# A recurrent attention and a GELU block in one launch: one list that orders all five queues is replaced by another

## The chip, the core and the metric

The kernel runs on one core of a Trainium2 chip. A core has five engines that matter here: TensorE (PE, matrix products; its weight loads are shown as PEld), VectorE (DVE), ScalarE (ACT), GpSimd (POOL) and SyncE (SP, which here only issues DMAs). Each engine works through a queue of its own, in order; semaphores hold an instruction until its inputs are there. The metric is the device time in microseconds (us) of one execution, the median over several runs.

## The reference, cut to what matters

```python
# r, k, v, w, a, b: (B, H, S, D) = (4, 8, 768, 40)
for t in range(S):
    y[:, :, t] = einsum('bhd,bhde->bhe', rt, state)
    Sa = einsum('bhde,bhe->bhd', state, at)
    state = state * wt[:, :, None, :] - einsum('bhd,bhe->bhde', Sa, bt)
    state = state + einsum('bhd,bhe->bhde', vt, kt)
x = y.transpose(0, 2, 1, 3).reshape(B * S, H * D)      # 3072 x 320
h = x @ w_in                                           # 320 x 2048
g = 0.5 * h * (1 + erf(h / sqrt(2)))
out = g @ w_out                                        # 2048 x 320
```

The two weights arrive as float64 and are converted to float32 on the chip.

## The kernel before, in words

**Tiling.** The sequence of 768 is cut into 12 chunks of 64 steps. Within a chunk the recurrence is turned into products: a triangular matrix is inverted, the state enters and leaves through products, and the 256 rows of y that a chunk gives (4 batches of 64) go through the GELU block at once. All products are in float32.

**Steps.** The kernel is written as about a hundred small functions, each marked as a step and each issuing instructions of mostly one engine. A token such as mh.3.6 calls step mh with the arguments 3 and 6; the first argument is the chunk, or the unit of a weight. `manual_schedule` is on for all five engines, so the order in which the steps are called is the order of the instructions on each engine's queue. That order is a list of 1450 tokens, written out in `order()` (line 19), and the kernel's last loop calls them one after the other:

```python
    for token in order(NCH, NS):
        perform(steps, token)
```

The list fixes the order of each queue only. Between queues the semaphores decide, and a step waits at the head of its queue for all that it reads and for the buffers that it writes.

**The steps that the text names**, with the engine and the line of the profile:
- Loads on SP: Lw, La, Lb, Lk, LV, Lr and others fetch a chunk's inputs (L447 to L515), Lf and Ls the weights (L537, L577).
- Weights, in units u (0 to 17 here): ce (two ACT instructions, L611 and L612), cs (two on DVE, L626 and L627), cm (DVE, L619) and cv (two on DVE, L635 and L636), in some units with cl, cn, cg, cx, cy in their place on other engines. A unit is usable after its cv.
- Decays: lg (ACT, L685, a logarithm), cu (PE), lt, ew, en, ec (ACT, exponentials and scalings), sb, sa, sk, sn (DVE or POOL) and the transposes ta, tb, tk, tv, tr (PE, or DVE as STREAM_TRANSPOSE). Chunks differ in the engine.
- The chunk's matrices: nm, vm, am (PE, L193), drained with a mask by nk, vk, ak (DVE); vc, rc, kc (ACT) drain transposes.
- The inverse: nd, nx, iz, then ic on POOL, about 30 us a chunk (L961, L963), then wx, tc_, wa, wb, and the products jm, km with the copies jc, kt0, kt1. For chunk 0 the inverse is made of squarings, qm on PE with qc, qb, qa, qz, qi on the other engines.
- The state: av, xm (PE), xc0 and xc1 (ACT or DVE copies, L1154), sm (PE), sc (DVE, L1175), pk, pb (PE), oa, od, om (DVE). oc, ot (ACT) and tn (DVE) turn the state for the next chunk; ym (PE) and yc (ACT, L1192 and L1194) give the part of y that comes from the old state.
- The GELU block: ox.c.0 and ox.c.1 move halves of y between partitions by five or six DMAs on SP (L1245, L1248). mh.c.p (PE, L1309) is one of eight products x @ w_in, with 20 matmuls; two of them fill a bank, which ge.c.q (ACT, L1314) reads with the GELU. For chunk 0, pm and pc multiply by w_out. From chunk 1 on, the product with w_out is made of seven products m1 to m7 (PE, L1348) with the sums ws, s1 to s4 (DVE), e1 to e6 (DVE and ACT). so and sz store the output through SP.
- Start: identity, sums_mask, upper_mask and the like set constants, most of them on POOL; warm and warm_first are products whose results nobody reads.

**PSUM.** Four tiles of two banks are handed out in the order of the list: a step on PE takes the tile that has been free longest, and the step that drains it gives it back. So the order of the drains on ACT and DVE decides when PE may go on.

```python
    def take(name, readers=1):
        held[name] = idle.pop(0)
    ...
    def drop(name):
        left[name] -= 1
        if not left[name]:
            idle.append(held.pop(name))
```

**ACT's tables.** A function of another kind than the one before needs a table load of 1.28 us on ACT (ACT_TABLE_LOAD in the profile); the order of the steps on ACT decides how many there are.

Of the kernel before, what the change touches and what calls it, by code (L numbers as in the profile page):

```python
# [18 lines left out]
def order(chunks, first_seven):  # L19
    return """  # L20
        first_ones.1 Lw.1 stripes_set identity pads_extra.1 sums_mask Lw.0 pads_r.1 warm.4.20 upper_mask
        pads_extra.3 La.0 pads_a.1 warm.4.0 pads_VR.1 pads_VR.0 of_half_set Lb.0 bias_set warm.4.13 pads_r.0 lg.1
        first_ones.0 pads_w.0 pads_rows.0 warm.4.25 pads_extra.0 Lb.1 pads_rows.1 onward_set lg.0 pads_w.1 wT.1
        pads_a.0 pads_extra.2 La.1 wT.0 warm.4.2 ew.1 Lf.0.1.0 ta.0 Lf.1.1.0 cu.0 Lf.0.0.0 cu.1 ec.0 Lf.1.0.0
        ew.0 sb.0 tb.0 sa.0 Lk.0 warm.4.15 sn.0 ec.1 nm.0 sb.1 Lf.2.0.0 warm_set tb.1 nk.0 Lf5.0.0 ta.1 sn.1 qt
        parity_set iz.1 sa.1 qm.0 qi.0.p qi.1.v nm.1 qz.0 warm_first ce.1 Lf.3.0.0 nk.1 qb.0.0.v Lf.3.1.0 qc.0
        cs.1 qb.0.1.a nd.1 qm.1 sk.0.p ce.0 nx.1 Lr.0 cm.1 Tt_zero tk.0 cs.0 cn.1 ic.1.0.4 qc.1 Lf.2.1.0 cl.1
        cx.1 qz.1 kc.0 Lf5.0.1 qb.1.0.v qa.1 qb.1.1.a cm.0 cy.1 ic.1.4.8 qm.2 Lf.0.0.1 cv.0 ce.3 LV.0 warm.4.18
        qz.2 am.0 qb.2.0.v qa.2 cs.3 ic.1.8.12 tr.0 Lf.1.0.1 ce.2 ak.0 Lw.2 qb.2.1.a cs.2 qc.2 Lf.0.1.1 rc.0 qm.3
        Lk.1 ic.1.12.16 Lf.2.0.1 qa.3 qz.3 Lf5.1.1 tv.0 qb.3.0.v qb.3.1.a cm.3 cm.2 cv.3 qm.4 vc.0 ic.1.16.20  # L30
        vm.0 qa.4 ql warm.4.4 vk.0 lg.2 Lf.2.1.1 ce.5 cv.2 av.0 Lf.3.1.1 ic.1.20.24 qc.3 qx jm.0 sk.1.v warm.4.24
        cs.5 Lf.1.1.1 cm.5 cv.5 Lf5.1.0 jc.0 km.0 xc0.0 xc1.0 ic.1.24.28 ce.7 Ls.3 cu.2 kt1.0 Ls.4 cs.7 kt0.0
        cm.7 sm.0 ic.1.28.31 cv.7 LV.1 ec.2 pk.0 sc.0.0 Lr.1 ce.9 sc.0.1 tk.1 cs.9 Lb.2 pb.0 kc.1 cm.9 cv.9 ce.4
        La.2 tv.1 om.0.1 om.0.0 Ls.2 cs.4 cm.4 Lf.3.0.1 vc.1 tr.1 od.0.1 cv.4 ox.0.0 am.1 rc.1 unused.v wT.2 ce.6
        sb.2 warm.4.1 one_set od.0.0 wx.1 ew.2 ta.2 ox.0.1 tb.2 sa.2 vm.1 sn.2 cs.6 cl.6 cm.6 nm.2 vk.1 oc.0 cn.6
        mh.0.0 nk.2 ot.0.1 cg.6 ot.0.0 ak.1 Ls.1 nd.2 Ls.0 nx.2 mh.0.1 iz.2 ce.8 tn.0 LV.2 unused.a mh.0.2 wb.1
        cs.8 ic.2.0.4 Lk.2 cm.8 cv.8 ge.0.0 av.1 Ls.6 ce.11 ym.1 ce.10 cs.11 ic.2.4.8 Ls.5 mh.0.3 tc_.1 Lr.2
        cm.11 yc.1 sk.2.v xm.1 cs.10 Ls.7 ge.0.1 cm.10 tv.2 ic.2.8.12 Ls.9 xc1.1 cv.10 xc0.1 Ls.10 jm.1 vc.2
        cv.11 Ls.8 tr.2 ce.12 tk.2 Ls.11 mh.0.6 ce.13 cs.12 ic.2.12.16 La.3 cm.12 kc.2 cs.13 mh.0.7 wa.1.1 cm.13
        jc.1 cv.12 rc.2 am.2 vm.2 cv.13 ic.2.16.20 ce.14 pm.0.0 Ls.13 cl.14 cs.14 Ls.12 ce.15 cm.14 ak.2 Lw.3  # L40
        cn.14 cs.15 km.1 wa.1.0 cg.14 vk.2 pm.0.1 kt1.1 ta.3 kt0.1 Ls.15 cm.15 Ls.14 cv.15 ic.2.20.24 ce.16 Lbt.3
        sm.1 ge.0.3 cs.16 ce.17 mh.0.4 sc.1.0 Lwt.3 sc.1.1 cl.17 ic.2.24.28 cm.16 mh.0.5 cs.17 Lr.3 cm.17 lg.3
        cv.16 pk.1 cn.17 cg.17 pb.1 ge.0.2 oa.1.0 cu.3 Lk.3 oa.1.1 pm.0.3 ec.3 od.1.0 Lw.4 ic.2.28.31 od.1.1 oc.1
        tw.3 ot.1.0 om.1.1 sk.3.p ot.1.1 om.1.0 av.2 tn.1 ox.1.1 pc.0.1 lt.3 ym.2 wx.2 iz.3 pm.0.2 tc_.2 yc.2
        unused.r pw.3 so.0.1 ew.3 tb.3 ox.1.0 jm.2 wb.2 en.3 pc.0.0 xm.2 jc.2 sn.3 km.2 xc0.2 tr.3 mh.1.0 xc1.2
        La.4 sa.3 wa.2.1 kt1.2 wa.2.0 nm.3 kt0.2 so.0.0 sm.2 nk.3 Lkt.3 mh.1.1 nd.3 sc.2.0 nx.3 lg.4 Lv.3 pk.2
        sc.2.1 ic.3.0.4 pb.2 ge.1.0 tk.3 mh.1.6 ic.3.4.8 oa.2.0 Lr.4 ta.4 mh.1.7 ws.0 LV.3 ws.1 mh.1.4 ge.1.3
        Lbt.4 ic.3.8.12 tr.4 mh.1.5 oa.2.1 Lk.4 kc.3 mh.1.2 tv.3 od.2.0 Lwt.4 ic.3.12.16 mh.1.3 od.2.1 oc.2
        om.2.0 vm.3 Lb.3 ge.1.1 am.3 ge.1.2 vk.3 m1.1 ot.2.1 ic.3.16.20 s1.1 ot.2.0 om.2.1 m2.1 s2.1 ox.2.1 ak.3
        m5.1 e1.1 tn.2 ws.3 av.3 e3.1 ic.3.20.24 s3.1 Lkt.4 ym.3 e2.1 tw.4 m6.1 yc.3 s4.1 ox.2.0 m3.1 ws.2 lt.4  # L50
        tk.4 m7.1 ic.3.24.28 e4.1 LV.4 tb.4 m4.1 e5.1 Lr.5 ic.3.28.31 xm.3 e6.1 pw.4 so.1.1 mh.2.6 xc0.3 La.5
        wx.3 ew.4 tc_.3 cu.4 sb.3 jm.3 en.4 so.1.0 mh.2.7 wb.3 sn.4 Lv.4 wa.3.0 jc.3 xc1.3 wa.3.1 km.3 sa.4 ec.4
        mh.2.4 sk.4.p tr.5 ge.2.3 kt1.3 Lkt.5 iz.4 ta.5 kt0.3 nm.4 sm.3 nk.4 Lw.5 mh.2.5 nd.4 nx.4 sc.3.0
        ic.4.0.4 mh.2.2 sc.3.1 Lbt.5 tv.4 mh.2.3 ic.4.4.8 kc.4 Lb.4 pk.3 ge.2.1 Lwt.5 ge.2.2 tb.5 pb.3 mh.2.0
        ic.4.8.12 sb.4 oa.3.1 oa.3.0 mh.2.1 od.3.0 om.3.1 am.4 ge.2.0 ic.4.12.16 om.3.0 vm.4 od.3.1 ox.3.1 m1.2
        s1.2 lg.5 tw.5 oc.3 ot.3.0 m2.2 s2.2 s4.2 m5.2 Lv.5 e1.2 vk.4 lt.5 ic.4.16.20 ot.3.1 s3.2 m6.2 ox.3.0
        ak.4 pw.5 m3.2 e3.2 ew.5 m7.2 La.6 e2.2 ic.4.20.24 tn.3 en.5 e4.2 m4.2 e5.2 av.4 e6.2 tk.5 so.2.1
        ic.4.24.28 ym.4 sn.5 Lr.6 mh.3.6 yc.4 sa.5 tv.5 LV.5 xm.4 ic.4.28.31 cu.5 xc1.4 xc0.4 mh.3.7 ec.5 wx.4
        tc_.4 wa.4.1 iz.5 ta.6 nm.5 ge.3.3 vm.5 Lbt.6 tr.6 wb.4 jm.4 nk.5 mh.3.2 jc.4 nd.5 Lwt.6 wa.4.0 nx.5
        mh.3.3 kc.5 ic.5.0.4 Lkt.6 vk.5 km.4 ge.3.1 mh.3.0 kt1.4 ic.5.4.8 kt0.4 tb.6 La.7 am.5 sm.4 tw.6  # L60
        ic.5.8.12 mh.3.1 lt.6 Lk.5 sc.4.1 sc.4.0 Lw.6 ak.5 mh.3.4 ge.3.0 pw.6 ic.5.12.16 mh.3.5 Lv.6 pk.4 ge.3.2
        s1.3 pb.4 so.2.0 lg.6 av.5 oa.4.1 ic.5.16.20 oa.4.0 m1.3 od.4.1 od.4.0 om.4.0 oc.4 m2.3 om.4.1 ot.4.0
        s2.3 ox.4.1 ot.4.1 ic.5.20.24 m5.3 tn.4 e1.3 s4.3 ew.6 ym.5 e2.3 s3.3 m6.3 yc.5 LV.6 tk.6 en.6 xm.5
        ic.5.24.28 ox.4.0 m3.3 xc0.5 ta.7 e4.3 sn.6 e3.3 m7.3 ic.5.28.31 Lk.6 sa.6 tv.6 Lb.5 m4.3 e5.3 Lbt.7 vm.6
        e6.3 nm.6 vk.6 mh.4.6 Lwt.7 nk.6 wx.5 wb.5 tc_.5 iz.6 mh.4.7 kc.6 nd.6 so.3.1 xc1.5 Lr.7 mh.4.2 nx.6 sb.5
        ic.6.0.4 ge.4.3 jm.5 am.6 jc.5 wa.5.1 km.5 wa.5.0 tw.7 sk.5.p mh.4.3 kt0.5 tb.7 ic.6.4.8 kt1.5 La.8
        mh.4.0 ak.6 ge.4.1 sm.5 Lb.6 ic.6.8.12 mh.4.1 sc.5.1 tr.7 pk.5 sc.5.0 ge.4.0 Lkt.7 ic.6.12.16 pb.5 lt.7
        cu.6 oa.5.1 Lw.7 mh.4.4 oa.5.0 pw.7 ic.6.16.20 mh.4.5 LV.7 om.5.1 m1.4 ge.4.2 Lv.7 od.5.0 om.5.0 s1.4
        m2.4 ec.6 ox.5.1 s2.4 ic.6.20.24 m5.4 od.5.1 ew.7 s3.4 en.7 s4.4 m6.4 oc.5 sn.7 ot.5.0 so.3.0 ot.5.1 m3.4
        sa.7 Lk.7 nm.7 e1.4 ox.5.0 ic.6.24.28 e3.4 e2.4 m7.4 e4.4 tn.5 m4.4 e5.4 ic.6.28.31 av.6 e6.4 nk.7 so.4.1  # L70
        sk.6.p ym.6 sb.6 wx.6 mh.5.6 wb.6 tv.7 iz.7 nd.7 tk.7 yc.6 mh.5.7 nx.7 Lr.8 wa.6.1 ic.7.0.4 vm.7 ge.5.3
        xm.6 Lwt.8 vk.7 mh.5.2 ic.7.4.8 xc0.6 ta.8 kc.7 Lbt.8 mh.5.3 xc1.6 tc_.6 tr.8 mh.5.0 ic.7.8.12 ge.5.1
        Lkt.8 tb.8 jm.6 lg.7 am.7 jc.6 Lb.7 wa.6.0 km.6 ic.7.12.16 tw.8 mh.5.1 so.4.0 kt1.6 ak.7 kt0.6 lt.8 Lv.8
        mh.5.4 pw.8 ic.7.16.20 ge.5.0 sm.6 mh.5.5 sc.6.0 sc.6.1 pk.6 ge.5.2 s1.5 pb.6 Lk.8 cu.7 oa.6.1 m1.5 La.9
        om.6.1 oa.6.0 ec.7 m2.5 sk.7.p od.6.0 om.6.0 s2.5 ox.6.1 m5.5 ic.7.20.24 e1.5 od.6.1 s3.5 oc.6 ew.8 m6.5
        s4.5 en.8 e2.5 m3.5 LV.8 e3.5 ot.6.0 e4.5 sa.8 ot.6.1 ox.6.0 m7.5 tn.6 ic.7.24.28 tk.8 m4.5 e5.5 Lr.9
        ic.7.28.31 av.7 e6.5 sb.7 sn.8 ym.7 so.5.1 mh.6.2 yc.7 wx.7 tc_.7 iz.8 Lb.8 xm.7 nm.8 mh.6.3 nk.8 nd.8
        tv.8 mh.6.6 xc1.7 Lwt.9 ge.6.1 nx.8 mh.6.7 kc.8 ic.8.0.4 Lw.8 vm.8 ge.6.3 am.8 xc0.7 vk.8 jm.7 ic.8.4.8
        wa.7.1 tw.9 mh.6.4 ta.9 lt.9 Lv.9 jc.7 pw.9 wb.7 mh.6.0 ic.8.8.12 lg.8 Lbt.9 wa.7.0 km.7 mh.6.1 kt1.7
        ak.8 kt0.7 ic.8.12.16 sm.7 ge.6.0 mh.6.5 sc.7.1 sc.7.0 tb.9 cu.8 ge.6.2 ic.8.16.20 Lw.9 pk.7 s1.6 pb.7  # L80
# [1388 lines left out]
```

## Time and profile before

| | |
|---|---|
| median of 3 runs | 647.54 us (647.45 to 648.93) |
| profiled execution, its own time | 648.82 us |
| its span | 646.9 us |
| TensorE busy | 617.4 us, 95% of the span |
| DVE, POOL, ACT busy | 457.3 (71%), 379.6 (59%), 323.9 us (50%) |
| mean granted TensorE clock | 0.99 |
| DMA | 64.3 MB, mean 99 GB/s |

A row of the time line gives the start and the duration in us, the engine, the line, the operation, what it writes and reads, the shape, and how often it stands in that row; in square brackets is the idle time of the engine before it and what ended that. A row of the windows gives the stretch, its length, the busy time of PE, PEld, DVE, ACT and POOL with the instructions, the granted clock, the share of the DMA engines and GB/s. A row of the groups gives the instructions of one line and form with their count, the busy time in us, the mean in ns, and the idle time before them. A row of the waits gives the engine and line that waited, what it waited for, the sum in us, how often, and the longest.

### The profile page before, as it was taken

What the parts mean: (1) busy time and instruction counts of PE and PEld (TensorE: products, weight loads), DVE (VectorE), ACT (ScalarE), POOL (GpSimd) and SP (SyncE); (2) the same over time, 40 slices, a digit from 0 to 9 for tenths busy, and PEclk for the clock granted to TensorE, in tenths of its full rate; (3) what the DMA queues carried; (4) which work ended last, traced back from release to release, by engine and by line L of the source; (5) the groups of instructions that cost most, each with busy time, mean ns of one, the idle gap of its engine ahead of it and who ended that gap; (6) DMA issues with size and microseconds to landing.
All of it is one profiled execution on the core that took longest, in us unless ns stands there. A gap on an engine that the chain in (4) does not pass through costs nothing.

```text
span 646.9 us, 31736 instructions
## 1 busy us (share of the span) xinstructions
PE 617.4 (95%) x14338; PEld 530.9 (82%) x14338; DVE 457.3 (71%) x557; ACT 323.9 (50%) x456; POOL 379.6 (59%) x782
## 2 busy tenths in 40 slices
...
GB/s 132 183 174 153 119 187 165 133 107 131 98 137 135 63 101 151 77 136 86 110 80 149 65 96 113 70 88 143 94 74 128 25 48 89 38 28 4 32 13 20
DMA packets 246914, 64.31 MB, mean 99 GB/s; under 512 B 228380, under 2 KB 243644, under 8 KB 246780
## 3 DMA queue, kind: packets, MB, share of 16 engines
...
q10 hardware_dynamic: 440, 0.29, 0.2%
q14 instruction: 22, 0.18, 0.1%
...
## 4 chain that ended last, share of the span: by engine, by line
PE 74%; issue 2%; ACT 2%; DVE 1%; DVEq 0%; ACTq 0%
PE bank L1309 29%; PE bank L1348 26%; PE bank L193 18%; DVE kT L721 0%; ACT L1314 0%; ACT L734 0%; ACT spare L922 0%; ACT T L942 0%; ACT Tt L937 0%; DVE spare L864 0%; ACT wpT L734 0%; ACT st L1194 0%; ACT kT L738 0%; ACT gt L1314 0%; DVE Tt L932 0%
## 5 line engine op out<-in xcount | busy, mean ns | idle before, releaser
L1309 PE MATMUL bank<-xt,w_in_sb 64*64 64x256 f32 x3840 | 224.5, 379 | 6.7 <-issue 6.0
L961 POOL TENSOR_TENSOR tmp<-W,Nb 128x126 f32<-128x126 f32 (+22 forms) x341 | 162.8, 478 | 95.3 <-DVE Nb L927 69.7
L1309 PEld LDWEIGHTS bank<-xt,w_in_sb 64*64 64x64 f32 x3840 | 161.3, 133 | 52.0 <-issue 11.1
L963 POOL TENSOR_TENSOR W<-W,tmp 128x126 f32<-128x126 f32 (+22 forms) x341 | 169.0, 496 | 26.7
L1348 PE MATMUL bank<-w_out_sb,gt 128*128 128x160 f32 x704 | 101.1, 301 | 0.0
L1314 ACT ACTIVATE gt<-bank 128x1024 f32<-128x1024 f32 x48 | 48.8, 1025 | 99.5 <-PE bank L1309 99.4
L1348 PEld LDWEIGHTS bank<-w_out_sb,gt 128*128 128x128 f32 x704 | 96.6, 190 | 2.3 <-issue 1.3
L1175 DVE TENSOR_TENSOR SM<-bank,upper 128x832 f32<-128x832 f32 (+1 forms) x24 | 23.0, 988 | 27.0 <-PE bank L193 25.8
L1263 ACT COPY conv<-st 32x128 f32<-32x128 f32 (+2 forms) x55 | 28.0, 510 | 17.6 <-DVE st L1257 15.9
L1227 DVE TENSOR_TENSOR st<-bank,st 128x832 f32<-128x832 f32 (+1 forms) x22 | 21.2, 986 | 14.4 <-PE bank L193 14.4
L1299 DVE TENSOR_TENSOR conv<-gt 128x1024 f32<-128x1024 f32 x11 | 14.1, 1280 | 24.3 <-ACT gt L1314 24.2
L1348 PE MATMUL bank<-extra,conv 128*128 128x160 f32 x208 | 30.3, 300 | 0.0
L1299 DVE TENSOR_TENSOR os<-os,bank 128x160 f32<-128x160 f32 x44 | 13.8, 314 | 21.8 <-PE bank L1348 20.1
L1348 PEld LDWEIGHTS bank<-extra,conv 128*128 128x128 f32 x208 | 28.9, 190 | 0.1
L721 DVE TENSOR_TENSOR_SCAN kT<-spare,kT 128x256 f32<-128x256 f32 x36 | 25.5, 766 | 0.8 <-ACT kT L714 0.7
L1348 PE MATMUL bank<-extra,gt 128*128 128x160 f32 x176 | 25.8, 300 | 0.0
L1348 PEld LDWEIGHTS bank<-extra,gt 128*128 128x128 f32 x176 | 24.5, 190 | 0.1
L789 POOL TENSOR_TENSOR bk_rows<-bk_rows,part 128x640 f32<-128x640 f32 x9 | 14.9, 1659 | 15.0 <-ACT part L742 13.4
L193 PE MATMUL bank<-SM,Tt 64*64 64x104 f32 (+1 forms) x768 | 20.6, 248 | 1.8 <-issue 1.5
L193 PEld LDWEIGHTS bank<-SM,Tt 64*64 64x64 f32 x768 | 19.0, 133 | 3.7 <-issue 2.3
L1314 ACT ACT_TABLE_LOAD x17 | 21.8, 1283 | 0.3
L1348 PE MATMUL bank<-extra,SM 128*128 128x160 f32 x144 | 21.2, 300 | 0.0
...
## 6 DMA issues: line engine op xcount, KB each, us to landing
...
```

The costliest lines, as they stand in the source:

```text
L193: nc.tensor.matmul(o, lhsT, rhs, start=first, stop=True, skip_group_check=True)
L721: nc.vector.tensor_tensor_scan(logs[:, at:at + n], onward, logs[:, at:at + n], 0.0, ALU.mult, ALU.add)
L789: (nc.vector if q == "v" else nc.gpsimd).tensor_tensor(to, rows(k_of(c)), decays(c), ALU.mult)
L961: nc.gpsimd.tensor_tensor(t, W[:, BL // 2 - rows:, rest:rest + 1].to_broadcast([P, rows, rest]), Nb[:, rest:rest + 1, :rest].to_broadcast( ...
L963: nc.gpsimd.tensor_tensor(own, own, t, ALU.add)
L1175: nc.vector.tensor_tensor(SM[:, g, :, :, cols], pair_of(f"S{c}_", g).rearrange("p x i c -> p i x c")[:, :, :, cols], kept, ALU.mult)
L1227: nc.vector.tensor_tensor(to, pair_of(f"QY{c}_", g)[:, :, :, cols], to, ALU.add)
L1263: nc.scalar.copy(apart.rearrange("p e i g d -> p (e i g) d")[to_rows, :, to_col:to_col + n], st.rearrange("p e i g c -> p (e i g) c")[rows ...
L1299: nc.vector.tensor_tensor(to, one_, other, how)
L1309: nc.tensor.matmul(ph[half(x ^ y), x, s], w_in_sb[half(x), kt, at:at + HP], xt[half(x), kt], start=kt == 0, stop=kt == NK - 1, skip_group_ ...
L1314: nc.scalar.activation(gt[:, 4 * q:4 * q + 4].rearrange("p (x s) t -> p x s t", x=2), bank(f"ph{c}_{q}").rearrange("p x (s t) -> p x s t", ...
L1348: nc.tensor.matmul(po[:, n, :DM // 2], l_[:, f], r_[:, f], start=f == 0, stop=f == NF // 2 - 1)
```

## The change

The list in `order()` is replaced. Both lists have the same 1450 tokens, each once; no step, shape, engine, tile or buffer differs, and the same matmuls, DVE and POOL instructions and DMAs are issued. Because the functions on ACT come in another order, the table loads go from 48 to 55. All later lines of the changed file are four lower, since the list is four lines shorter. The old list stands above; of the new one, the parts that the prediction speaks of:

```diff
 def order(chunks, first_seven):
     return """
-        first_ones.1 Lw.1 stripes_set identity pads_extra.1 sums_mask Lw.0 pads_r.1 warm.4.20 upper_mask
...
+        pads_rows.0 pads_r.0 stripes_set pads_VR.1 identity warm_set warm_first pads_extra.0 sums_mask warm.4.4
+        bias_set Lw.1 lg.1 warm.4.0 Lw.0 Lb.0 La.0 warm.4.2 warm.4.18 Lb.1 cu.1 lg.0 pads_extra.2 cu.0 upper_mask
+        Lf.1.1.0 pads_w.0 ec.0 sb.0 pads_a.0 wT.0 ew.0 tb.0 sn.0 ec.1 ta.0 pads_w.1 parity_set wT.1 first_ones.0 sa.0
+        nm.0 pads_extra.1 sb.1 ew.1 tb.1 nk.0 qt first_ones.1 qi.1.v pads_a.1 Lf.1.0.0 ce.1 La.1 pads_r.1 sn.1 qm.0
+        qc.0 ta.1 cl.1 warm.4.13 qz.0 Lk.0 of_half_set qi.0.p qb.0.0.v cs.1 sa.1 cm.1 qb.0.1.a qm.1 qa.1 qz.1 Lf.0.1.0
...
+        ic.1.8.12 qb.3.0.v qa.3 qb.3.1.a qm.4 Lr.0 tr.0 Lw.2 ic.1.12.16 cs.2 cm.2 cv.3 ak.0 vc.0 lg.2 Lf.0.0.1
+        ic.1.16.20 rc.0 qa.4 ql ic.1.20.24 vm.0 cv.2 jm.0 vk.0 av.0 Lf.0.1.1 ce.5 cs.5 cm.5 cv.5 qx ic.1.24.28 Lf5.0.0
+        Lf.2.0.1 Lr.1 xc1.0 Lf5.1.1 jc.0 km.0 kt1.0 LV.1 xc0.0 ce.7 kt0.0 cu.2 ec.2 cs.7 warm.4.1 cm.7 cv.7 sm.0
+        sc.0.0 sc.0.1 tv.1 Lf5.1.0 ce.9 cs.9 ce.4 pk.0 pb.0 cm.9 cv.9 vc.1 tr.1 Lf.1.1.1 om.0.0 om.0.1 Lf.1.0.1 od.0.0
+        Lb.2 ic.1.28.31 cl.6 od.0.1 wT.2 rc.1 vm.1 sb.2 La.2 Lf.3.1.1 ta.2 oc.0 ot.0.0 tb.2 ew.2 cs.4 sn.2 cm.4 cv.4
+        sa.2 Lk.1 ce.6 ox.0.1 sk.1.v cs.6 warm.4.25 pads_extra.3 Lf.3.0.1 ot.0.1 cm.6 nm.2 nk.2 tk.1 cn.6 unused.a
+        tn.0 ox.0.0 mh.0.0 cg.6 mh.0.1 wx.1 iz.2 mh.0.2 kc.1 Ls.2 Ls.3 nd.2 nx.2 vk.1 am.1 ce.8 cs.8 cm.8 cv.8 Ls.1
+        ak.1 mh.0.3 ce.11 cs.11 ge.0.0 av.1 ic.2.0.4 cm.11 Ls.0 ce.10 ym.1 ge.0.1 Lk.2 sk.2.v tk.2 yc.1 xm.1 xc0.1
+        unused.v LV.2 tv.2 tc_.1 kc.2 cs.10 cm.10 cv.10 cv.11 Ls.5 Ls.4 ce.12 jm.1 jc.1 ic.2.4.8 cs.12 cm.12 cv.12
+        mh.0.6 mh.0.7 Ls.6 vc.2 wb.1 Ls.7 ce.13 Lr.2 tr.2 Ls.8 cs.13 cm.13 cv.13 pm.0.0 Ls.9 ic.2.8.12 wa.1.0 xc1.1
+        ce.14 cs.14 cm.14 Ls.11 ic.2.12.16 rc.2 vm.2 vk.2 cl.14 cn.14 Ls.10 ce.15 am.2 ak.2 km.1 ic.2.16.20 kt0.1
...
+        wx.2 wa.2.1 wa.2.0 om.1.1 ox.1.0 wb.2 tn.1 pc.0.1 tw.3 lt.3 ym.2 tb.3 yc.2 tc_.2 pw.3 ew.3 iz.3 en.3 pm.0.2
+        Lr.3 pc.0.0 sa.3 jm.2 sn.3 jc.2 ox.1.1 xm.2 xc1.2 mh.1.0 km.2 kt0.2 kt1.2 Lv.3 nm.3 mh.1.1 unused.r La.4 tr.3
...
+        tr.5 mh.2.3 ge.2.1 od.3.1 mh.2.0 mh.2.1 oa.3.0 od.3.0 am.4 ic.4.16.20 Lwt.5 ic.4.20.24 vm.4 so.1.0 sk.4.p tb.5
+        ic.4.24.28 ic.4.28.31 om.3.1 LV.4 om.3.0 tw.5 ge.2.2 vk.4 ge.2.0 m1.2 m2.2 s1.2 s4.2 s2.2 s3.2 m5.2 m6.2 oc.3
...
```

In words: the old list mixes the queues finely, roughly as the instructions run; the new one more often puts a step right behind the one that it reads from, and whole rows of the same unit or chunk together (cs, cm, cv of a unit; the parts of ic).

More of the change, by code (lines that the diff above doesn't have):

```diff
@@ L20, in order @@
     return """
-        first_ones.1 Lw.1 stripes_set identity pads_extra.1 sums_mask Lw.0 pads_r.1 warm.4.20 upper_mask
[L22 to L80, printed above, removed]
@@ L96, in order @@
-        en.11 ic.10.24.28 mh.9.3 sn.11 sa.11 mh.9.6 e5.8 ge.9.1 mh.9.7 e6.8 ic.10.28.31 so.8.1 so.8.0 nm.11 wx.10
-        ge.9.3 iz.11 av.10 wb.10 nk.11 Lr.11 ym.10 nd.11 wa.10.0 mh.9.4 tc_.10 yc.10 Lv.11 nx.11 wa.10.1
-        ic.11.0.4 mh.9.5 tr.11 Lkt.11 jm.10 ge.9.2 ic.11.4.8 xm.10 jc.10 cu.11 xc1.10 km.10 tv.11 mh.9.0
-        ic.11.8.12 ec.11 kt1.10 kt0.10 xc0.10 mh.9.1 ic.11.12.16 sm.10 ge.9.0 m1.9 sc.10.1 sc.10.0 tk.11 pk.10
-        ic.11.16.20 s1.9 pb.10 m2.9 oa.10.1 oa.10.0 om.10.0 m4.9 e1.9 sk.11.p om.10.1 s4.9 ox.10.1 m5.9 s2.9
@@ new lines, in order @@
+        m2.1 s4.1 Lw.4 ot.2.0 ot.2.1 ic.3.28.31 tn.2 om.2.0 LV.3 av.3 e1.1 ym.3 yc.3 pads_rows.1 Lwt.4 tw.4 Lb.4 m5.1
+        Lr.4 s2.1 s3.1 lt.4 Lk.3 tr.4 ws.3 e3.1 Lbt.4 wx.3 wa.3.0 xm.3 wb.3 m6.1 xc1.3 m3.1 ox.2.1 xc0.3 m7.1 lg.4
+        tc_.3 jm.3 jc.3 ws.2 m4.1 tb.4 km.3 e2.1 Lv.4 e4.1 e5.1 ox.2.0 kt0.3 Lkt.4 pw.4 e6.1 so.1.1 iz.4 La.5 mh.2.6
+        mh.2.7 wa.3.1 kt1.3 ew.4 sa.4 tv.4 sk.3.p cu.4 ec.4 sm.3 mh.2.4 mh.2.5 en.4 sn.4 ge.2.3 tk.4 sc.3.0 sc.3.1
+        nm.4 nk.4 Lk.4 ta.5 mh.2.2 kc.4 nd.4 nx.4 pk.3 ic.4.0.4 pb.3 ic.4.4.8 ic.4.8.12 ic.4.12.16 Lr.5 Lbt.5 oa.3.1
```

84 lines of the change are left out of this document (60 added, 24 removed).

## The prediction

> **What bounds the kernel now.** I read the page first (span and busy time), then the waits of TensorE, then busy time by stretch, and last the time line at the places where the new order differs most.
>
> ```profile
> span 646.9 us, 31736 instructions
> PE 617.4 (95%) x14338; PEld 530.9 (82%) x14338; DVE 457.3 (71%) x557; ACT 323.9 (50%) x456; POOL 379.6 (59%) x782
> ```
>
> ```profile
> PE bank L193 <- issue: 10.1, 9, 2.2
> PE bank L1309 <- issue: 6.0, 8, 1.2
> PE bank L193 <- POOL cum_m L360: 2.7, 1, 2.7
> PE bank L193 <- ACT Js L1091: 1.5, 1, 1.5
> ```
>
> ```profile
> 60.00:100.00 40.00, 39.35 (x1060) 32.57 (x1064) 34.77 (x57) 34.83 (x47) 24.16 (x50) 1.00 0.78 158
> ...
> 200.00:400.00 200.00, 192.93 (x4718) 172.28 (x4720) 157.03 (x175) 97.07 (x137) 140.58 (x286) 1.00 0.57 106
> ```
>
> TensorE is busy 617.4 of 646.9 us, and no product is added or removed, so the new order can save at most 29.5 us of idle time. Of these, 10.1 + 6.0 = 16.1 us are "issue", where nothing that the profile shows was awaited; I leave them as they are. About 13 us remain, with the first product's wait of 2.7 for the mask and km.2's of 1.5 for ACT among them. In 60 to 100 us TensorE works 39.35 of 40, while DVE and ACT are at 34.8 each: none of the three has room, and a step put behind the wrong neighbour on DVE or ACT is seen by TensorE at once. From 200 us on ACT is half idle and DVE works 157 of 200, so a bad place costs less there. The lists keep 1450 steps; the only instructions that change in number are ACT's table loads, 48 before and 55 after, since the functions now alternate more.
>
> **The method.** For each product I added the durations, from the time line of before, of the steps that stand between its inputs and the last product that they need, on the queues of the new order, and took away the TensorE work in the new list that covers it. What is left is a raw wait. Once TensorE has come late, the other queues have gained that time, so later waits shrink. I count small waits at half, and count in full the three with full queues around them.
>
> **The start (0 to 77 us).**
>
> ```profile
> 2.71 6.13 PE L193 MATMUL bank<-cum_m,ident 128*128 128x512 f32 x8 [2.71 <-POOL cum_m L360]
> ...
> 25.46 0.55 PE L193 MATMUL bank<-N,st 32*32 32x32 f32 x24 [2.20 <-issue]
> ...
> 27.85 4.65 PE L193 MATMUL bank<-w_in_sb 128*128 128x512 f32 x6
> 32.43 2.08 PE L193 MATMUL bank<-turned,st 64*64 64x64 f32 x64
> ```
>
> ```profile
> 22.31 0.35 POOL L949 COPY W<-parity 128x16 f32<-128x16 f32 x2 [13.34 <-DVE parity L408]
> ```
>
> Before, the 4.65 us of filler (warm_first) stood between the first and second squaring, with qm.1 at 32.43. After, the filler is the first product of all and needs only a DVE memset: an estimated start at 1.3 instead of 2.71. POOL's queue stood 13.34 us at iz.1, with qi.0.p behind it; after, qi.0.p is ahead of iz.1. tb.0 will wait some 1.9 us for sb.0 (ec.0 now follows cu.0) and qm.0 about as long as before. I get qm.1 at 27.4 (25.7 to 29.0): a gain of 5.0 us (3.4 to 6.7).
>
> Then the losses. vm.0 waits for a bank that rc.0 drains, now behind lg.2 with a table load: raw 1.3. av.0 follows with one short product between, and its input vk.0 is behind cv.2: 1.8. cu.2 needs the bank that xc1.0 frees, now behind cs.5, cm.5 and cv.5 on DVE: 2.8. The largest is mh.0.0.
>
> ```profile
> 66.44 0.60 SPq L537 DMA_DIRECT2D gt<-in_moe_w_in_dram  x1
> 68.01 0.90 SPq L1245 DMA_DIRECT2D xt<-xt  x1
> ...
> 73.48 2.45 SPq L1248 DMA_DIRECT2D xt<-xt  x4
> ```
>
> ```profile
> 76.77 5.60 PE L1309 MATMUL bank<-xt,w_in_sb 64*64 64x256 f32 x90
> ```
>
> The two halves of ox.0 took SP from 68.01 to 75.93, and mh.0.0 followed at 76.77 without a gap. After, a weight load (Lf.3.0.1, like the 0.60 row) stands between the halves, Lf.3.1.1 and Lk.1 ahead of the first; and among the products ahead of mh.0.0 tv.1 no longer follows om.0's products, am.1 is behind mh.0.0, and tk.1 comes in: an estimated 2.2 us less cover. Raw 4.4. The four sum to 10.3, at half 5.2 (full: 10.3). The start comes to -5.0 + 5.2 = +0.2 us, from 5.2 - 6.7 = -1.5 to 10.3 - 3.4 = +6.9.
>
> **The three large waits.** First pm.0.0, which needs unit 13 of w_out converted.
>
> ```profile
> 91.15 1.97 PE L193 MATMUL bank<-ident,VR 128*64 128x128 f32 x32
> ...
> 93.05 0.75 PE L193 MATMUL bank<-turned,spare 32*32 32x32 f32 x64
> 93.16 1.01 ACT L836 COPY late<-bank 128x1024 f32<-128x1024 f32 x1 [0.29 <-PE bank L193]
> ...
> 93.73 1.09 PE L751 MATMUL bank<-ident,r_pairs 128*128 128x128 f32 x8
> ...
> 94.07 0.91 ACT L611 ACTIVATE conv<-w_out_sb,rebias 128x640 int16<-128x640 int16 x1
> ...
> 95.62 4.55 PE L1309 MATMUL bank<-xt,w_in_sb 64*64 64x256 f32 x80
> ...
> 95.79 0.67 DVE L626 TENSOR_TENSOR conv<-conv 128x640 int16<-128x640 int16 x1 [0.46 <-ACT conv L612]
> ...
> 96.49 0.42 DVE L627 TENSOR_SCALAR conv<-conv 128x640 int16<-128x640 int16 x1
> ...
> 98.63 0.75 DVE L619 TENSOR_SCALAR conv<-w_out_sb 128x640 uint32<-128x640 uint32 x1
> ...
> 98.89 0.37 ACT L1091 COPY Js<-bank 128x256 f32<-128x256 f32 x1
> ...
> 101.25 1.08 DVE L635 SCALAR_TENSOR_TENSOR conv<-w_out_sb,conv 128x640 f32<-128x640 uint32 x1
> ...
> 102.36 0.93 DVE L636 SCALAR_TENSOR_TENSOR w_out_sb<-conv 128x640 f32<-128x640 f32 x1
> 102.67 0.35 PE L193 MATMUL bank<-rT,late 40*64 40x64 f32 x9 [0.75 <-issue]
> ```
>
> ```profile
> L942 ACT COPY T<-Tt 32x256 f32<-32x256 f32 x22 | 8.9, 402 | 17.8 <-DVE Tt L932 17.4
> L1154 ACT COPY SM<-bank 128x832 f32<-128x832 f32 x13 | 10.9, 852 | 8.2 <-PE bank L193 8.2
> ```
>
> After xm.1 ACT has in this order xc0.1 (0.85), kc.2 (1.0, like the 1.01 of vc), ce.12 (two of 0.91), jc.1 (0.37), vc.2 (1.01), wb.1 (two of 0.40) and ce.13 (1.82): 7.7 us; then DVE runs cs.13 (0.67 + 0.42), cm.13 (0.75) and cv.13 (1.08 + 0.93): 3.85, so 11.5 in all. TensorE has tv.2 (1.97), jm.1 (0.75), mh.0.6 and mh.0.7 (4.55) and tr.2 (1.09) in that time: 8.4. Before, am.2 and vm.2 also stood ahead of pm.0.0, with the conversion of unit 13 started earlier. The wait is 3.1, less the 0.75 that before lost at vm.2: +2.3 (1.7 to 2.9, since cm.13 runs beside ACT in part).
>
> Second mh.1.0, where before waited at km.2.
>
> ```profile
> 131.45 1.18 SPq L1418 DMA_DIRECT2D out_dram<-os  x2
> ...
> 136.09 2.90 SPq L455 DMA_DIRECT2D a_pairs<-in_a_dram  x4
> ...
> 137.84 0.26 PE L193 MATMUL bank<-Tt,Js 32*32 32x32 f32 x2 [1.53 <-ACT Js L1091]
> ```
>
> Between the halves of ox.1 stood so.0.1 (1.18); after it is Lr.3, four issues like the 2.90 row: 1.7 us later. mh.1.0 also moves ahead of km.2, so km.2's 1.53 overlaps it. Net +0.8 to +1.5: +1.1. Third xm.1: only tk.2 (1.0) now stands between ym.1 and xm.1, where yc.1 takes an estimated 1.75; before a whole mh stood there. +0.8. The three: +4.2.
>
> **The small waits.** km.1 behind vm.2 and the bank that vk.2 frees, 0.3; m4.1, whose ws.2 stands on DVE behind tc_.3 and so behind POOL's ic.3, 0.8 (0 to 1.8); nm.5, vm.5 and am.5, with sn.5 and sa.5 on DVE behind s1.2 to s4.2 and tn.3, 1.2; sm.4, with kt0.4 behind ge.3.1 and its table load, 0.6; m6.1 and jm.5, 0.8; jm.7 and nm.8, 1.0.
>
> ```profile
> L1314 ACT ACTIVATE gt<-bank 128x1024 f32<-128x1024 f32 x48 | 48.8, 1025 | 99.5 <-PE bank L1309 99.4
> L1314 ACT ACT_TABLE_LOAD x17 | 21.8, 1283 | 0.3
> ```
>
> sm.4 shows how these come about: 1.28 + 1.03 us stand ahead of its copy, and one mh (4.55 / 2 = 2.3, row above) covers them; the copy's own time is left over. The other extra table loads are off TensorE's path where ACT is half idle: nothing, or 1.28 each if the cover were gone. The sum is 4.7, at half 2.35 (0 to 4.7). Late in the kernel I find waits of 0.8 new and 1.1 gone: -0.3. The moves of SP's loads that I do not name have their data early by chunks: nothing.
>
> **The clock.**
>
> ```profile
> 24.70:31.50 6.80, 6.04 (x93) 3.79 (x93) 5.29 (x7) 3.41 (x6) 3.58 (x3) 0.50 0.80 160
> 137.30:140.80 3.50, 2.96 (x84) 2.18 (x88) 3.24 (x3) 3.43 (x7) 0.00 (x0) 0.51 0.80 158
> ```
>
> Twice the granted clock fell to half, for 6.8 and 3.5 us, each time beside a wait (2.20 and 1.53). A stretch of 3.5 us at half costs 1.75. I leave their number at two and put 1.75 for one more into the upper bound. The Trainium skill ("TensorE: Matmul & The Clock Gate", Part 1: The HAM clock gate) has the clock halve only after an idle window of about 3.4 us; by that none of the new waits would lower it. The row of 137.30 speaks against so strict a reading.
>
> **The sum.** 0.2 + 4.2 + 2.35 - 0.3 = +6.45, so +6.5 us. The profiled execution took 648.82 (span 646.9 and 1.9 around it) and would take 655.3; on the median of 647.54, which is 1.28 below it, that is 654.0. The case's own ends: -1.5 + 4.2 + 0 - 0.3 = +2.4 (649.9), and 6.9 + 4.2 + 4.7 - 0.3 = +15.5 (663.0), the clock's 1.75 lying just outside.
>
> **The rivals.** *A, faster.* The start's gain stands and what follows is absorbed. For it: the 13.34 us block on POOL and the filler are real, and from 200 us on DVE and ACT have room. Against: 60 to 100 us has none. Priced: -5.0, the start's losses at a quarter (+2.6), km.2's 1.5 gone, later waits zero, -0.3: -4.2, or 643.3. It decides if mh.0.0 starts before 73 us.
>
> *B, no change.* The waits shrink to what the start gives: -2.4 + 2.4, within 0.3% (1.9 us, about what a measurement of this kernel can tell from no change), 645.6 to 649.5.
>
> *C, much slower.* The ox transfers starve mh in the steady part. In six chunks (1 to 5 and 8) a load stands between the two halves of ox on SP; at 2.90 us each, uncovered, +17.4, or 665. Against: before has other transfers between them too, like the 1.18 row, and TensorE waited at none in 200 to 400 us, where it lost 7.1 in all, mostly issue.
>
> That the order on the queues does not change is excluded, since the list is the order.
>
> **How the numbers follow.** Forecast 0.62, A 0.18, B 0.11, C 0.09. Half of A lies below 644 and C above 663, which leaves out 0.18: range 644 to 663; the forecast's own is 649.9 to 663. Faster 0.18, same 0.11, slower 0.62 + 0.09 = 0.71.
>
> **What would show it.** The first product near 1.3 us; qm.1 near 27.4; mh.0.0 at 77 or later with a gap ahead of it that a DMA of xt releases; a gap of 2 to 4 us at pm.0.0 released by DVE's w_out_sb; one at mh.1.0 released by the DMA of xt; gaps under 1.5 us at nm.5, sm.4 and nm.8; issue again near 16 us. I am wrong if pm.0.0 and mh.1.0 show no gap (then A), if TensorE's idle time in 200 to 600 us grows by more than 6 us (then C), or if busy time of TensorE itself changes by over 3 us.

## The result: 1.3% slower, and the profile after

The new order took 656.92 us (median of 4; 655.26 to 657.15) against 647.54 before: ratio 1.0134, 95% interval 1.0113 to 1.0156, or 9.4 us more where 6.5 were forecast. The experiments ran in three groups, each beside the old list, which took 645.4 to 645.5 in all three; the new one, run again in the last (e12), took 656.9: ratio 1.0168 (1.0119 to 1.0216), 11.4 us more. Since the old list agrees, runs of all groups are compared with e12. An execution over 1.5% above the fastest of its kernel is left out of the times as slow, which happened once, in e9.

> The new list itself, beside the others on the same chip: 656.9 by the first job, or some 2 us less if this chip is like that of e1 to e8, where the old list took 645.4.

The profiled execution of after took 657.15 us itself. Its page, and TensorE's waits (engine and line, what it waited for, sum in us, times, longest):

```profile
span 655.3 us, 31779 instructions
...
PE 620.1 (95%) x14338; PEld 528.1 (81%) x14338; DVE 457.2 (70%) x557; ACT 333.7 (51%) x463; POOL 379.5 (58%) x782
...
PE 45%; POOL 9%; DVE 2%; issue 2%; ACT 1%; DMA 1%; SPq 0%; DVEq 0%; POOLq 0%; ACTq 0%
```

```profile
PE bank L189 <- DVE turned L1063: 6.6, 2, 3.7
PE bank L189 <- issue: 5.8, 4, 1.7
PE bank L189 <- DVE VR L860: 3.7, 3, 3.0
PE bank L747 <- POOL extra L375: 1.8, 1, 1.8
...
PE bank L1305 <- issue: 0.4, 2, 0.2
...
PE bank L1305 <- DMA xt<-xt: 0.3, 1, 0.3
```

TensorE idles 35.2 us instead of 29.5 and is busy 2.7 us longer. But the composition has turned over: issue fell from 16.1 to 6.2, of which 5.8 stand in the first 58 us, and the rest of the idle time rose by about 15.6. POOL, absent from the chain of before, now has 9% of the chain. The time line of TensorE says where (start, duration; in brackets the idle time before it and what ended that):

```profile
189.75 1.07 PE L189 MATMUL bank<-turned,spare 32*32 32x32 f32 x64 [2.87 <-DVE turned L1063]
192.13 4.60 PE L1344 MATMUL bank<-extra,gt 128*128 128x160 f32 x16 [1.32 <-DVE extra L1292]
...
293.03 1.07 PE L189 MATMUL bank<-turned,spare 32*32 32x32 f32 x64 [3.05 <-DVE VR L860]
...
346.53 0.93 PE L189 MATMUL bank<-turned,N 32*32 32x32 f32 x64 [3.75 <-DVE turned L1063]
```

These are jm.3, m4.1, jm.5 and jm.6. The releaser named for jm.3 and jm.6 is DVE's tc_, which has only passed on what it waited for: POOL's elimination ic ended at 187.4, 288.9 and 344.8, and jm followed within 1.7 to 4.1 us. jm.5 waited for a PSUM tile that vk.6 drains, and vk.6 stands on DVE's queue behind the same tc_.5. POOL's own queue shows why it ended late in chunks 5 and 6. The first step of ic.3, ic.4, ic.5 and ic.6 in after, then in before:

```profile
150.40 0.24 POOL L957 TENSOR_TENSOR tmp<-W,Nb 128x31 f32<-128x31 f32 x1 [18.94 <-DVE Nb L923]
...
214.03 0.24 POOL L957 TENSOR_TENSOR tmp<-W,Nb 128x31 f32<-128x31 f32 x1 [23.39 <-DVE Nb L923]
...
255.76 0.24 POOL L957 TENSOR_TENSOR tmp<-W,Nb 128x31 f32<-128x31 f32 x1 [2.22 <-DVE Nb L923]
...
308.91 0.24 POOL L957 TENSOR_TENSOR tmp<-W,Nb 128x31 f32<-128x31 f32 x1 [18.14 <-DVE Nb L923]
```

```profile
147.94 0.24 POOL L961 TENSOR_TENSOR tmp<-W,Nb 128x31 f32<-128x31 f32 x1 [17.70 <-DVE Nb L927]
...
200.54 0.24 POOL L961 TENSOR_TENSOR tmp<-W,Nb 128x31 f32<-128x31 f32 x1 [5.38 <-DVE Nb L927]
...
244.38 1.06 POOL L961 TENSOR_TENSOR tmp<-W,Nb 128x31 f32<-128x31 f32 x1 [5.92 <-DVE Nb L927]
...
290.37 0.66 POOL L961 TENSOR_TENSOR tmp<-W,Nb 128x31 f32<-128x31 f32 x1 [2.02 <-DVE Nb L927]
```

For chunk 6 POOL stood 18 us waiting for nx.6, where before it stood 2: nm.6 is at 303.8 us instead of 283.1, behind mh.4.0 and mh.4.1. For chunk 5 the delay comes from the chunk before: POOL stood 23 us waiting for nx.4 instead of 5, so ic.4 ended at 251.1 us instead of 236.7, and ic.5 could only follow. Chunk 3 is another case. POOL stood about as long as before, but from nm.3 to jm.3 TensorE has 41.0 us of work (first row, after) where it had 45.3 (second row, before), too little to cover the chain:

```profile
145.18:189.75 44.57, 41.01 (x954) 38.10 (x953) 31.97 (x32) 17.30 (x27) 33.81 (x68) 1.00 0.76 137
141.98:188.16 46.18, 45.33 (x1020) 41.63 (x1013) 38.73 (x43) 18.95 (x26) 33.81 (x62) 1.00 0.64 122
```

So an engine that is busy only 58% of the span became the bound in places: its idle time lay ahead of a chain of 33 to 37 us (chunks 3 to 11) that TensorE must wait out.

The granted clock adds to the loss. In the windows view (the granted clock stands behind the five busy times) the five stretches at half clock of after are:

```profile
22.60:29.40 6.80, 5.10 (x138) 4.02 (x138) 4.49 (x8) 1.89 (x3) 5.68 (x8) 0.50 1.19 190
77.20:84.00 6.80, 5.73 (x44) 3.86 (x48) 4.25 (x5) 4.29 (x7) 4.96 (x12) 0.50 0.51 143
189.80:196.60 6.80, 5.48 (x80) 5.11 (x80) 6.52 (x11) 1.73 (x3) 0.84 (x1) 0.50 0.01 2
292.20:299.00 6.80, 5.97 (x110) 5.58 (x114) 4.59 (x10) 0.91 (x3) 0.00 (x0) 0.50 0.19 40
346.80:350.20 3.40, 3.40 (x83) 2.26 (x72) 2.41 (x2) 2.91 (x5) 2.58 (x4) 0.50 0.68 106
```

30.6 us at half, against 10.3 before; each begins at one of the waits above or at the start's. m4.1 took 4.60 us in the third, where a product of its kind takes 2.3. What the clock cost by itself was not measured: 20.3 us more at half speed is at most 10 us of TensorE time, and its busy time rose by 2.7. A slow stretch can also be partly free. In e12, the same list, stretches at half stand in other places, TensorE is busy 622.1 us and comes later to jm.3 and jm.5, which wait 2.14 and 1.55 us there instead of 2.87 and 3.05; the time is the same.

### The profile page after: what moved, and what is told of

The parts are those of the page before. It is cut to its first block, busy times and chain, and to the rows that moved or that the text cites. A ratio compares the mean times of both kernels' runs of the same rounds, so it can differ in the third digit from the quotient of the medians.

```text
span 655.3 us, 31779 instructions
## 1 busy us (share of the span) xinstructions
PE 620.1 (95%) x14338; PEld 528.1 (81%) x14338; DVE 457.2 (70%) x557; ACT 333.7 (51%) x463; POOL 379.5 (58%) x782
## 3 DMA queue, kind: packets, MB, share of 16 engines
q8 instruction: 112, 1.84, 1.2%
## 4 chain that ended last, share of the span: by engine, by line
PE 45%; POOL 9%; DVE 2%; issue 2%; ACT 1%; DMA 1%; SPq 0%; DVEq 0%; POOLq 0%; ACTq 0%
PE bank L1305 18%; PE bank L1344 17%; PE bank L189 10%; POOL W L959 5%; POOL tmp L957 4%; DMA r_pairs<-in_k_dram 1%; ACT gt L1310 0%; DVE Nb L923 0%; DVE turned L1063 0%; SPq L451 0%; POOL bk_rows L785 0%; DVE Tt L928 0%; ACT L1310 0%; ACT L710 0%; DVE kT L753 0%
## 5 line engine op out<-in xcount | busy, mean ns | idle before, releaser
L957 POOL TENSOR_TENSOR tmp<-W,Nb 128x126 f32<-128x126 f32 (+22 forms) x341 | 162.4, 476 | 134.2 <-DVE Nb L923 108.7
L1305 PEld LDWEIGHTS bank<-xt,w_in_sb 64*64 64x64 f32 x3840 | 154.3, 135 | 52.8 <-issue 5.2
L959 POOL TENSOR_TENSOR W<-W,tmp 128x126 f32<-128x126 f32 (+22 forms) x341 | 168.2, 493 | 26.7
L1344 PE MATMUL bank<-extra,gt 128*128 128x160 f32 x176 | 30.7, 335 | 1.3 <-DVE extra L1292 1.3
L1344 PEld LDWEIGHTS bank<-extra,gt 128*128 128x128 f32 x176 | 28.4, 216 | 1.9 <-ACT Js L1087 1.4
L928 DVE STREAM_TRANSPOSE Tt<-W 128x512 f32<-128x512 f32 x11 | 7.6, 694 | 21.8 <-POOL W L959 21.8
L1344 PEld LDWEIGHTS bank<-extra,SM 128*128 128x128 f32 x144 | 20.0, 190 | 0.8 <-ACT os L1389 0.7
```

Of the source, the lines that this page charges most:

```text
L928: nc.vector.transpose(flat(Tt)[:, :, BL:].rearrange("p n (t q) -> p t n q", q=2), W_tile.rearrange("p (t n q) -> p t n q", n=NBL, q=2))
L957: nc.gpsimd.tensor_tensor(t, W[:, BL // 2 - rows:, rest:rest + 1].to_broadcast([P, rows, rest]), Nb[:, rest:rest + 1, :rest].to_broadcast( ...
L959: nc.gpsimd.tensor_tensor(own, own, t, ALU.add)
L1305: nc.tensor.matmul(ph[half(x ^ y), x, s], w_in_sb[half(x), kt, at:at + HP], xt[half(x), kt], start=kt == 0, stop=kt == NK - 1, skip_group_ ...
L1344: nc.tensor.matmul(po[:, n, :DM // 2], l_[:, f], r_[:, f], start=f == 0, stop=f == NF // 2 - 1)
```

## The experiments

**e1 and e2: the two lists spliced.** Both lists obey the same dependencies, so the first part of one can be followed by the rest of the other.

```diff
- for token in order(NCH, NS):                      # one list
+ e1: old list up to sm.6, then the tokens that remain in the new list's order
+ e2: new list up to sm.6, then the tokens that remain in the old list's order
```

> The old list up to sm.6 (chunk 6, at 354 us of the trace of before), then all remaining tokens in the order of the new list. Theory: the issue gaps are TensorE out of instructions (one packet of 256 each), and the new order has none of them in its second half because products with many short matmuls no longer stand together; from sm.6 to the end before lost 10.4 us of TensorE time and after 4.4, so 6.0 us less than before: 641.5 (640 to 643.5). Rival: the new order's own long waits earlier gave the instruction queue time to fill, and without them the gaps return: 647.5, within 1.5.

> The reverse: the new list up to sm.6, then the remaining tokens in the old order. Theory (instruction packets, a matter of the order on TensorE in the second half): 656.9 + 6.0 = 662.9 (661 to 665). Rival (the earlier waits filled the queue): 656.9, within 1.5.

e1 took 642.4 us: 0.9946 of before (0.9917 to 0.9975), the fastest complete order that was found. The time lies in the range expected, but that was reckoned from an old list at 647.5; beside the 645.5 of its own group the gain is 3.1, half of the 6.0 expected. e2 took 661.7, 4.8 over e12, of 6.0 expected. So the second half of the new order is better than that of the old, by 3 to 5 us, and the first half costs more than the whole difference. From 366 us on, by the windows view (TensorE's busy time is the first of the five):

```profile
366.00:514.00 148.00, 146.82 (x3621) 127.86 (x3617) 110.29 (x127) 81.99 (x111) 95.90 (x192) 1.00 0.56 105
```

```profile
366.00:514.00 148.00, 144.02 (x3456) 126.92 (x3452) 109.85 (x126) 75.73 (x106) 88.40 (x183) 1.00 0.55 103
```

The first is after, the second e2 with the same first half. After issues 3621 matmul rows in these 148 us, e2 3456. The rival of e1, that the gaps come back once the long waits ahead of them are gone, falls: behind sm.6 e1 has one issue gap, 0.81 us at 358.9.

**e3: one memset earlier.** tk.1 waited 1.82 us for pads_extra.3, which the new list puts behind ic.1 on POOL.

```diff
-  ... ic.1.28.31 pads_extra.3 ...
+  ... pads_extra.1 pads_extra.3 ...
```

> The new list with one token moved: pads_extra.3 (a memset on POOL) from behind ic.1.28.31 to behind pads_extra.1. Theory: tk.1 waited 1.82 us for it, and the clock fell to half for 6.8 us from 77.2 on because of that wait and the 0.9 before it, worth 3.4 more: 652 to 655, if both go. Rival: mh.0.0 behind it waits for ox.0 anyway, so the time is 656.9 within 1.

657.1 us: nothing gained. No wait stands at tk.1, and mh.0.0 behind it waited instead, at 82.24 us:

```profile
82.24 6.83 PE L1305 MATMUL bank<-xt,w_in_sb 64*64 64x256 f32 x120 [2.76 <-DMA xt<-xt]
```

The rival was right about the time: ox.0 is late there, as the prediction had it for mh.0.0, and a wait ahead of it that it outlasts is free. The trace alone does not show what the edit did. e12, without it, has no wait at tk.1 either, and mh.0.0 waits 1.65 us there; in both the clock fell earlier, at 56.7 to 63.6 us in e3 and 56.9 to 63.7 in e12, so that TensorE came to tk.1 later than in after.

**e4: POOL's chain cut short in chunks 3, 5 and 6.**

```diff
-  ic.3.16.20 ic.3.20.24 ic.3.24.28 ic.3.28.31     (the same in chunks 5 and 6)
```

> The new list without the last 15 of the 31 elimination steps on POOL in chunks 3, 5 and 6 (twelve tokens ic.c.16.20 to ic.c.28.31 left out, so the inverse of these chunks is incomplete and the output is not the reference's). Theory: jm.3, jm.5 and jm.6 waited 2.87, 3.05 and 3.75 us for POOL's chain, and the clock was at half for 17 us behind them, worth up to 8.5: without these 9.7 + 8.5 = 18.2, some of it given back as issue gaps of 0.7 to 1.7 each: 643 (639 to 647). Rival: DVE or the transfers are late at the same places anyway (ws.2 for m4.1, the late buffers): 652 or more.

641.7 us, 15.2 less than e12; ratio 0.9942 to the old list (0.9906 to 0.9979). jm.3, jm.5 and jm.6 follow without a wait, and the clock no longer falls at 190, 292 and 347 us. The row of jm.3:

```profile
185.01 0.75 PE L188 MATMUL bank<-turned,spare 32*32 32x32 f32 x64
```

So the late end of the elimination in these three chunks, with what follows from it, accounts for more than the whole of what the change cost. The same cut in the old list was not run; there no product but the first waits for POOL, by the waits of its trace.

**e8: the old start.** The old list up to pm.0.0, then the new order.

> The old list up to pm.0.0 (103 us), then the remaining tokens in the new order. At equal work done, after was 4.4 us behind before at km.1. Theory: the start's loss is passed on whole, since POOL's inverse of chunk 3 begins only after nm.3: 652.5 (651 to 654). Rival: it is absorbed in the later waits for POOL: 656.9, within 1.

651.7 us, 5.2 less than e12: the start's loss is passed on whole. This 5.2 and the 15.2 of e4, less the 3 to 5 us of the better second half, come to more than the 11.4 that the change costs here: the parts are not independent, and no run has both edits.

**e11: one chain moved earlier.**

```diff
-  sn.6 kc.6 Lr.7 jc.5 km.5 kt0.5 kt1.5 ox.4.0 mh.4.0 iz.6 mh.4.1 ge.4.0 La.7 nm.6 nk.6 nd.6 nx.6 ic.6.0.4
+  sn.6 nm.6 nk.6 kc.6 Lr.7 jc.5 km.5 iz.6 nd.6 nx.6 kt0.5 kt1.5 ic.6.0.4 ox.4.0 mh.4.0 mh.4.1 ge.4.0 La.7
```

> The new list with nm.6, nk.6 directly behind sn.6, and iz.6, nd.6, nx.6 behind km.5, so that POOL's inverse of chunk 6 begins 5 to 6 us earlier. Theory (POOL's chain began too late for jm.6): the wait of 3.75 at jm.6 and the 3.4 us at half clock behind it go: 651.5 (650.5 to 654). Rival (chunk 6 would wait for something else at the same place, or the gain is given back by chunk 7): 656.9 within 1.5.

656.6 us: the rival. The elimination began 3.9 us earlier and jm.6 no longer waits (345.66 us), but nm.6 now waits 1.55 for sn.6 and the clock falls behind it (302.0 to 305.4), and at 387 to 391 us two new waits of 1.37 and 0.50 stand. One chain set right in an order whose neighbours are laid for the late one gives nothing. That e4 gained because all three chunks had room at once is my reading, not shown.

```profile
299.86 1.16 PE L189 MATMUL bank<-aT,nT 40*64 40x64 f32 x64 [1.55 <-DVE nT L801]
```

**e5, e6, e7, e9, e10: what issue is.** The page of before has 112 packets of instructions on queue 8, 1.84 MB:

```profile
q8 instruction: 112, 1.84, 1.3%
```

1.84 MB / 112 is 16 KB. TensorE has 2 x 14,338 instructions (products and weight loads), 28,676 / 112 = 256 to a packet, so these are TensorE's own; e9, with 30,596 of them, has 120 packets. By the records of that queue, all 14 issue gaps over 0.5 us that before has from 100 us on end 1.3 to 1.6 us after a packet has landed, for example:

| gap of TensorE, us | instructions begun before it | last packet, us |
|---|---|---|
| 434.01 to 434.52 | 19,815 | 431.76 to 433.17 |
| 446.08 to 447.13 | 20,583 (3 x 256 more) | 444.78 to 445.71 |
| 488.60 to 490.27 | 22,369 (7 x 256 - 6 more) | 487.70 to 488.66 |
| 542.76 to 543.49 | 24,922 (10 x 256 - 7 more) | 540.87 to 541.98 |

e2, which ends as before does, has its four gaps there after 19,811, 20,579, 22,365 and 24,918 instructions: the same packet boundaries, at other times. In the 5 us up to their ends TensorE had begun 327 to 423 instructions, where 28,676 in 646.9 us are 222 on average.

```diff
+ e5: in the old list, an mh between jm.9, km.9, nm.10; likewise in chunks 4 to 8 (20 tokens moved)
+ e6: in the new list, vm, vk, am, ak of chunks 7, 8, 9 directly ahead of pk.6, pk.7, pk.8
+ e7: old list with the moves of e5 up to pb.6, jc.2 ahead of en.3, then the new order
```

> The old list with 20 tokens moved a few places, so that products of 64 short matmuls (nm, vm, am, jm, km) no longer follow each other: at seven places an mh (40 matmuls in 2.2 us) stands between two of them. Theory: the issue gaps stand where TensorE uses up a packet of 256 instructions before the next has come; eight gaps of before stand at these places (242.8, 251.8, 288.0, 296.5, 351.5, 395.6, 447.1 and 490.3 us, 8.6 us in all) and go, a few tenths come back elsewhere: 3 to 8 us less than before in the same job, most likely 5. Rival: the packets come late because of the data transfers, whatever TensorE does; the gaps move to other packets: within 1.5 us of before.

> The new list, with vm and am of chunks 7, 8 and 9 (and vk and ak that drain them) moved to stand directly ahead of pk.6, pk.7 and pk.8, so that four products of 64 matmuls (512 instructions with their weight loads) run in 4.7 us. Theory (packets): three new issue gaps of 1 to 2.2 us at these places, where after had none: 661 (659 to 664). Rival: no issue gap appears there, as after's second half has none at any place; a wait for a PSUM tile at pk shows at most: 656.9, within 1.5.

> A version meant to beat both: the old list with the moves of e5 in chunks 4 to 6 and jc.2 moved ahead of en.3 on ACT (km.2 waited 1.5 us for jc.2, and the clock fell behind it), up to pb.6, then the new order. From 642.4 of e1 the gaps at 283.9 (0.86) and 291.6 (1.61), km.2's 1.52 and some 1.5 of the transition go: 638 (636 to 641). If the packets theory and that of the second half are wrong: 642 to 646.

In these three, am of two or three chunks comes behind the step tw that overwrites its input; number and kind of the instructions are the same. e5 took 643.8, 0.9965 of before (0.9939 to 0.9990), 1.6 us less than the old list beside it, where 3 to 8 were expected and the rival allowed 1.5. In its trace issue fell to 8.3 us, and 5.6 us more than in before stand as waits for ACT and DVE.

```profile
PE bank L188 <- issue: 4.5, 7, 2.0
PE bank L1304 <- issue: 3.8, 7, 0.8
```

e6 took 664.6, 7.7 over e12, but the three issue gaps that its theory forecast did not come. Its two new gaps (1.50 at 374.1 and 2.33 at 423.8 us) are waits for a drain on DVE: they end 0.50 and 1.27 us after the last packet landed, after 16,309 and 18,597 instructions, which is not where a packet ends by the counts above. So products of 64 short matmuls side by side need not bring an issue gap, and the time of e6 does not speak for the theory. e7 took 643.0, no better than e1, and so fell where its expectation put it if the theories were wrong. Its trace has 6.6 us of issue, e1's 7.0: the gap at 291.6 went, but others (1.58 at 141.3, 1.03 at 244.5) came. The pair e9 and e10 measures the cost by itself, in an order that has no such gaps after chunk 6:

```diff
 def products(name, lT, rT, swap):
     pt = take(name)...
+    e9:  chunks 7 to 11: the loop over the 64 short matmuls runs twice
+    e10: chunks 7 to 11: mm(bank(name)[:, 0], ident, cum_m...) first, one long product
```

> The new order; in chunks 7 to 11 the 64 short matmuls of nm, vm and am are issued twice (same operands, same tile, same result): 15 times 0.93 us more work on TensorE and 128 more instructions each time, so 256 instructions in 1.9 us. Theory (packets of 256 instructions): besides 14 us of work, issue gaps of 0.5 to 2 us at most of the 15 places, where after had none: 681 to 690, and some 10 to 20 us above e10. Rival (issue has to do with the data transfers or with waits elsewhere): the same as e10 within 1.5.

> The new order; in the same 15 places one long product (128x128 by 512 columns, two matmul rows, about 1.02 us, overwritten by the product behind it) is added instead: the same work on TensorE with 4 instructions. Both theories: 656.9 + 15 x 1.0 = 672 (669 to 673), no issue gaps beyond those of after.

e9 took 682.9 us (median of three; 680.8 to 685.2), e10 674.1, which is 1.1 above its range: 8.8 apart for work on TensorE that was chosen to be about the same, where 10 to 20 were expected. The waits, e9 first. Its only profile is of an execution of 691.8 us, so its gaps may be longer than in the three others:

```profile
PE bank L190 <- issue: 12.5, 12, 1.8
```

```profile
PE bank L190 <- issue: 4.1, 3, 1.9
```

From 355 us on e9 has eight issue gaps, 0.56 to 1.83 us long, each ending 1.3 to 1.7 us after a packet landed; e10 has none of that kind. So issue is TensorE out of instructions, and how often it comes depends on how many instructions the order asks for in a few microseconds. How many it takes was not found, and a gap that goes need not be worth its length: from the trace of before to those of e1 and e5 issue fell by 9.1 and 7.9 us, and the time by 3.1 and 1.6.

## Why the prediction was right, point by point

The sign, the range (644 to 663) and the size within a factor of 1.5 held, 9.4 us against 6.5. That the size came so near was luck: the waits that made the loss were mostly not those of the sum, and issue, which was left alone, fell by 10 us against them.

**The start: inside its range, its parts wrong.** The term was +0.2 (-1.5 to +6.9); behind the same 2,282 products km.1 begins at 111.88 us instead of 107.45, and e8 measures +5.2. The first product came at 1.52 and qm.1 at 29.73 us, not 27.4: a gain of 2.7 instead of 5.0. Of the four losses, vm.0 waited 1.10 (raw 1.3), av.0 0.29 (1.8), cu.2 not at all (2.8), and mh.0.0 (4.4) not in after, where tk.1 ahead of it waited 1.82, but 1.65 in e12. These sum to less than the halves that were counted. In their place stand issue, 5.8 us up to km.1 instead of 3.9, and small waits that the sum did not have. TensorE's busy time up to km.1 is the same (96.1 and 96.3 us). pads_extra.3 behind ic.1 on POOL, a step past which it was moved, was overlooked.

**The three large waits: wrong.** They were to cost 4.2. pm.0.0 and xm.1 show no wait, because TensorE came to them 2 to 6 us later (the half clock at 77.2 to 84.0 had slowed mh.0.0), and ACT and DVE had that time. mh.1.0 waited 0.31. They would have needed the halving that the small waits got. The prediction had said that without gaps at pm.0.0 and mh.1.0 rival A, faster, would hold. That sign was wrong: the gaps were all but gone, and the new order was slower.

```profile
143.85 0.66 PE L1305 MATMUL bank<-xt,w_in_sb 64*64 64x256 f32 x6 [0.31 <-DMA xt<-xt]
```

**The small waits: the step that failed.** m4.1 behind tc_.3 and so behind ic.3 was named, at 0.8 (0 to 1.8); it waited 1.32, but jm.3 ahead of it, which was not in the list, waited 2.87. jm.5 was in a pair at 0.8 and waited 3.05; jm.6 was not in the list and waited 3.75. The raw wait of jm is what is left of a chain that begins at nm, some 42 to 52 us earlier, and the text ahead of the prediction puts ic at about 30 us, the busy time of its instructions. In the groups of after's page:

```profile
L957 POOL TENSOR_TENSOR tmp<-W,Nb 128x126 f32<-128x126 f32 (+22 forms) x341 | 162.4, 476 | 134.2 <-DVE Nb L923 108.7
...
L959 POOL TENSOR_TENSOR W<-W,tmp 128x126 f32<-128x126 f32 (+22 forms) x341 | 168.2, 493 | 26.7
```

162.4 + 168.2 over 11 chunks is 30.1 us a chunk, but from its first instruction to its last ic takes 33 to 37 us from chunk 3 on. For chunk 3: 5.2 us from nm.3 (145.2) to ic, 37.0 of ic and 2.3 to jm.3 make 44.5, and TensorE is busy for 41.0 of them; of the 3.5 that are missing 2.87 are the wait that the row shows. sm.4, nm.5 and nm.8 show no wait. The remark that a bad place costs less from 200 us on, read from the shares of ACT and DVE, missed this: the two longest waits stand there.

**Issue: wrong.** It was left at 16.1 us and fell to 6.2. e1 and e2 measure the better second half at 3 to 5 us, so the change would have cost more without it; how much for the issue gaps alone is open. That the gaps went because the new order puts an mh between products of 64 short matmuls fits e9 against e10 and the fall of issue in e5, but e6 did not bring them back by bunching.

**The clock: wrong by rows that stood in the prediction.** Two stretches were forecast and there were five, 20.3 us more at half speed, up to 10 us of TensorE time. The reading of the row at 137.30, that a wait of 1.5 us can be enough, was right, and the upper bound had room for one such stretch only. It is not always enough: issue gaps of 1.65 and 1.67 us in before (at 294.9 and 488.6) and 1.74 in after (at 55.8) brought none. The strict rule of the Trainium skill ("TensorE: Matmul & The Clock Gate", Part 1: The HAM clock gate), an idle window of about 3.4 us, disagrees with the falls at waits of 1.5 to 3.1; that the stretches last 3.4 or 6.8 us, one or two windows, agrees with it.

**Rival C's sign in 200 to 600 us.** TensorE's busy time there moved from 388.8 to 390.2 us, so the idle time did not grow, and by the waits of after no transfer starved mh in the steady part.
